# A cosine layer with six Strassen pairs of chunks, and three of its elementwise operations on GpSimd

## The chip, the cores and the metric

The kernel runs on one core of a Trainium2 chip. The metric is the device time of one execution in microseconds, median over several runs; before the change it is 544.96 us (3 runs, 544.89 to 545.14).

## The reference, cut to what matters

Attention (2 batches, 12 heads, 448 tokens, head size 64, causal mask), then a gated layer of 768 x 1536, then the layer that the change is about:

```python
def _moe2_ref(x, w_in, w_out):          # x: 896 x 768, w_in: 768 x 2048
    h = x @ w_in
    g = h * np.cos(h)
    return (g @ w_out).astype(np.float32)
```

The weights come as 64-bit floats, and the result is wanted in 32-bit precision.

## The kernel before

**Layout.** All activations lie transposed: 128 features on the partitions, 448 tokens of one batch on the free axis. Batch b is one moving operand of 448 columns. Each fp32 operand is held as a rounded part (hi) and a remainder (lo), and each 128 x 128 block of weights is multiplied three times (hi by hi, hi by lo, lo by hi): these are the lines L232 to L234 in `products`, and L500 to L502 in `Product.product`.

**Weights.** A chunk is 128 rows of outputs by 768 inputs. SyncE loads it as raw 64-bit words. ScalarE takes the upper part out (L169), VectorE puts the fp32 word together (L171; `upper_of` and `word_of`), ScalarE makes hi (L467, called by `parts`) and VectorE lo (L429, called through `difference` by `low`).

**The cosine layer.** Its 16 chunks of weights go in eight pairs, u = 0 to 7, called units here. `KINDS` says how each is done. A plain unit (P) multiplies two chunks with two batches: 8 halves (numbers 8 to 15) of 9 matmuls, 72 in all. A Strassen unit (S) takes the 2 x 2 blocks (two chunks by two halves of the inputs, and two halves of the inputs by two batches) with seven products (numbers 1 to 7) of 9 matmuls, 63 in all. Product 4 of an S unit is issued in the unit behind it (`old`). So a unit behind an S unit has 9 more matmuls than its own order has, and an S unit has 54 of its own besides.

An S unit needs sums of the weights. With f0 and f1 the words of its chunks: s1 = f1 left half + f1 right half and s2 = s1 - f0 left half (`sums12`, L478 and L479 by way of L429, in the unit before it), s3 = f0 left - f1 left and s4 = f0 right - s2 (`sums34`, L481 to L485), hi of the left block of them by ScalarE, lo by VectorE. In PSUM, ScalarE copies product 1 (L527) into the bank in which products 6 and 7 add up, and later that bank again (L536); VectorE adds s5 to it behind product 6 (L533) and behind product 7 (L538). L538 writes `tmp`, in SBUF: it is one of the unit's four results. The other three stay in PSUM.

**Order.** The schedule is written out by hand: each engine runs its instructions in the order in which the loop emits them. A unit has a position `at` for each product in `order`; `emit` issues that product on TensorE, then the work behind the one before it (`behind`). Then come pieces of the work on weights by position, then one step of `cosines`: it finishes the result that was begun a position ago (ScalarE's sine L736, VectorE's product with h L737) and begins another (ScalarE's scaled copy L742, VectorE's remainder L743). In an S unit behind an S unit the order on VectorE is: s3, s4 and a remainder (at 0); word of f0 of the next unit, low22 (L493), product, remainder of `tmp` (at 1); lo of s3 and s4, product with `tmp` (at 2); lo of the next A, remainder (at 3); L533, word of f1 of the next unit, s1, s2, product (at 4); remainder (at 5); L538, lo of s1 and s2, product (at 6). On ScalarE: hi of the lower right block (L489), upper part, copy; L527, hi of s3 and s4, sine, copy of `tmp`; L530, hi of the next A, sine of `tmp`; upper part, copy; sine; hi of s1 and s2, copy; L536, sine. GpSimd has work in the attention alone (L290, L286, and the sum L362 of two SBUF operands of 448 columns).

The lines that matter:

```python
for at, n in enumerate(order):
    emit(old if n == 4 else unit, n)
    if at == 0:
        if seven:
            unit.sums34()
            unit.high22()
```

Of the kernel before, what the change touches and what calls it, by code (L numbers as in the profile page):

```python
# [18 lines left out]
ALU = mybir.AluOpType  # L19
# [3 lines left out]
B, H, S, D = 2, 12, 448, 64  # L23
# [14 lines left out]
WH = KP * P  # L38
PLAIN = 2

KINDS = "PSSPSSSP"

FIRST_ROWS = {2: (0, 3), 4: (3, 5)}
FIRST_ROWS_END = 5
# [29 lines left out]
def attn_moe_moe2(  # L74
# [9 lines left out]
    nc = tc.nc  # L84
# [16 lines left out]
    def slot(tag, name, dtype=F32R):  # L101
        pool = gpool if tag[0] == "g" else spool if tag[0] == "t" else hpool if tag in ("f0", "f1", "f2") else bpool
        return pool.tile([P, 2, S], dtype, tag=tag, name=name)
# [313 lines left out]
    def temp(tag, bufs):  # L417
        return epool.tile([P, S], F32, tag=tag, name=tag, bufs=bufs)
# [9 lines left out]
    def difference(dst, a, b):  # L428
        nc.vector.tensor_tensor(dst, a, b, op=ALU.subtract)  # L429
# [19 lines left out]
    def run(n):  # L449
        for i in range(n):  # L450
            next(todo, None)
# [8 lines left out]
    class Product:  # L460
# [17 lines left out]
            nc.vector.tensor_tensor(s1, f1[:, :WH], f1[:, WH:], op=ALU.add)  # L478
            difference(s2, s1, f0[:, :WH])  # L479

        def sums34(self):  # L481
            f0, f1 = self.w
            self.s34 = slot("t14", "s34", F32).rearrange("p a s -> p (a s)")[:, : WC * P]
            difference(self.s34[:, :WH], f0[:, :WH], f1[:, :WH])
            difference(self.s34[:, WH:], f0[:, WH:], self.s12[:, WH:])  # L485

        def high22(self):
            self.a22 = epool.tile([P, 2, WH], F32R, tag="a22", name="a22", bufs=2)
# [53 lines left out]
    class Gate(Product):  # L542
# [5 lines left out]
        def result(self, n):  # L548
            if n == 2:
                self.sg0 = temp("sg", 4)  # L550
                nc.scalar.activation(self.sg0, self.a[:, :S], AF.Sigmoid)
            elif n == 3:
                sg1 = temp("sg", 4)
                nc.scalar.activation(sg1, self.c[:, :S], AF.Sigmoid)
                gated(self.f, 1, sg1, self.tmp)
            else:
                gated(self.f, 0, self.sg0, self.e[:, :S])

    for f in range(PLAIN):
# [18 lines left out]
        if f == PLAIN - 1:  # L578
            unit = Gate(PLAIN)
# [25 lines left out]
    def upper_of():  # L605
        k = Chunk(step("decode"))
        k.decode(0, 0, k.n)
        return k

    def word_of(k):  # L610
        k.decode(1, 0, k.n)
        load_chunk()
        return k.w
# [3 lines left out]
    def emit(u, n):  # L617
        u.p(n)
        if done:
            v, m = done.pop()  # L620
            v.behind(m)
        done.append((u, n))
# [3 lines left out]
    for f in range(PLAIN, KH):  # L626
# [31 lines left out]
        unit, old = new, unit  # L658
# [68 lines left out]
    GF = [None] * KG  # L727
    GFTAG = ["t5", "t6", "t7", "t8", "b6", "b7", "b8", "t9", "t10", "t11", "g2", "g3", "f4", "f5", "f6", "t12"]
    due, turned = [], []

    def cosines():
        if turned:
            h, r, (f, b) = turned.pop(0)
            if GF[f] is None:
                GF[f] = slot(GFTAG.pop(0), f"g{f}", F32)
            nc.scalar.activation(r, r, AF.Sin, scale=TWOPI, bias=quarter)  # L736
            nc.vector.tensor_tensor(GF[f][:, b], r, h, op=ALU.mult)  # L737
        if due:
            h, fb = due.pop(0)
            r = temp("sg", 4)  # L740
            n = r.bitcast(I32)
            nc.scalar.activation(n, h, AF.Copy, scale=INV2PI, bias=0.25)  # L742
            nc.vector.scalar_tensor_tensor(r, h, INV2PI, n, op0=ALU.mult, op1=ALU.subtract)  # L743
            turned.append((h, r, fb))

    GTAG = ["b4", "f7", "b0", "b5", "f8", "b1", "t3", "f9", "b2", "t4", "t13", "t14"] + sum(XTAG, [])
    GORD = [(k, b) for c in range(0, KG, WC) for b in range(B) for k in range(c, min(KG, c + WC))]
# [3 lines left out]
    def split_g(n):  # L751
        for i in range(n):
            if GORD:
                k, b = GORD.pop(0)
                G[b][k] = slot(GTAG.pop(0), f"g{k}{b}")
                split(G[b][k], GF[k][:, b])
                if b == B - 1 and GFREE:
                    GTAG.append(GFREE.pop(0))

    class Pair(Product):  # L760
# [17 lines left out]
        def result(self, n):  # L778
            f = self.f
            if n == 2:  # L780
                due.append((self.a[:, :S], (f, 0)))
            elif n == 3:
                due.extend([(self.c[:, :S], (f, 1)), (self.tmp, (f + 1, 1))])
            elif n == 4:
                due.append((self.e[:, :S], (f + 1, 0)))
            elif n % 2:
                i, b = (n - 8) // 4, (n - 8) // 2 % 2
                due.append((self.banks[i, b][:, :S], (f + i, b)))

    c3 = at_chunk["use"]  # L790
    unit, old = Pair(0), None
    unit.A = next_chunk()
    unit.w = None, singles.pop(c3 + 1).w
    for u, kind in enumerate(KINDS):
        new, last = Pair(u + 1), u == len(KINDS) - 1
        seven = kind == "S"
        new_seven = not last and KINDS[u + 1] == "S"
        if seven:
            order = (1, 5, 2, 6, 4, 7, 3) if old else (1, 5, 6, 2, 7, 3)
        else:  # L800
            order = (8, 9, 4) + tuple(range(10, 16)) if old else tuple(range(8, 16))
        for at, n in enumerate(order):
            emit(old if n == 4 else unit, n)
            if at == 0:
                if seven:
                    unit.sums34()
                    unit.high22()
                else:
                    unit.C = unit.parts(unit.w[1])
                k0 = upper_of()  # L810
            elif at == 1:
                w0 = word_of(k0)
                if seven:
                    unit.S34 = unit.parts(unit.s34)
                    unit.low22()
                else:
                    unit.low(unit.C, unit.w[1])
            elif at == 2:
                new.A = unit.parts(w0)
                if seven:  # L820
                    unit.low(unit.S34, unit.s34)
            elif at == 3:
                k1 = upper_of()
                unit.low(new.A, w0)
            elif at == 4:
                new.w = w0, word_of(k1)
                if new_seven:
                    new.sums12()
            elif at == 5 and new_seven:
                new.S12 = new.parts(new.s12)  # L830
            if at == min(len(order) - 1, 6) and new_seven:
                new.low(new.S12, new.s12)
            cosines()
            run(1)
            if last and at > 1:
                split_g(1)
        unit, old = new, unit if seven else None
# [9 lines left out]
    for j in range(KP):  # L847
        ps2 = [[bank() for i in range(2)] for b in range(B)]
        for c in range(nch):
            wts = [next_chunk()]  # L850
            for b in range(B):
                advance()
                for i in range(2):
                    if i and not b:
                        wts.append(next_chunk())
                    g, m = G[b][c * WC : min(KG, c * WC + WC)], 2 * j + i
                    products(ps2[b][i], wts[i], g, c == 0, c == nch - 1)
                    cosines()
                    split_g(3)
                    if c == nch - 1:  # L860
                        o, ps = temp("sg", 4), ps2[b][i]
                        rows, c0 = slice(m * P, m * P + P), b * S
                        if m == KX - 1 and b == B - 1:

                            nc.scalar.copy(o[:, : S // 2], ps[:, : S // 2])
                            nc.vector.tensor_copy(o[:, S // 2 :], ps[:, S // 2 : S])
                            nc.scalar.dma_start(out=out[rows, c0 : c0 + S // 2], in_=o[:, : S // 2])
                            nc.sync.dma_start(out=out[rows, c0 + S // 2 : c0 + S], in_=o[:, S // 2 :])
                        else:
                            nc.scalar.copy(o, ps[:, :S])  # L870
                            nc.sync.dma_start(out=out[rows, c0 : c0 + S], in_=o)
# [55 lines left out]
```

## Time and profile before

| | |
|---|---|
| median of the runs | 544.96 us |
| the profiled execution's own time | 545.12 us |
| its span, first to last instruction | 543.3 us |
| around the span | 1.8 us |
| granted TensorE clock, mean | 1.000 |
| matmuls | 3059 |
| the cosine layer's units 0 to 6, first matmul to first matmul of unit 7 | 317.76 to 408.30 us |

The profile is one execution on the chip. Times are counted from the start of the span. PE is TensorE, DVE VectorE, ACT ScalarE, POOL GpSimd. A row of the timeline has the start in us, the duration in us, engine, line, operation, output and inputs with their shapes, and in brackets the idle time in front of it with what ended that. Instructions of one engine overlap: the next can start before the last has ended, so that the distance of two starts is what an instruction costs its engine when it is busy, and start plus duration is when another engine can go on.

### The profile page before, as it was taken

Reading aid. Unit: us, or ns where it says so; the run is one execution under the profiler, and the core shown is the slowest. Engines: PE = TensorE matmul, PEld = TensorE weight load, DVE = VectorE, ACT = ScalarE, POOL = GpSimd, SP = SyncE. Lnnn points to the kernel's source line nnn. Section 1 sums busy time; section 2 is a strip of 40 time slices with the busy share of each in tenths; the row PEclk is TensorE's granted clock in tenths of the full one; section 3 lists DMA queues with packets and bytes.
Section 4 is the critical chain, followed back from the end, with each engine's and each line's share of the span. In section 5 each row is a group of like instructions: output and inputs, shape, how many; then the busy total and the mean of one; then the engine's idle time right before and its main releaser. Section 6 shows DMA issues by size and latency. Waiting matters only on the chain.

```text
span 543.3 us, 8153 instructions
## 1 busy us (share of the span) xinstructions
PE 535.6 (99%) x3059; PEld 479.7 (88%) x3059; DVE 366.0 (67%) x688; ACT 321.4 (59%) x622; POOL 59.4 (11%) x131
## 2 busy tenths in 40 slices
PE   7999999999999999999999999999999999999997
PEld 5666679989999999999999999999999999999996
DVE  4889959896777777893626279977988991411400
ACT  5898956675555555882535277766787972513401
POOL 4688860000000000000000000000000000000000
PEclk9999999999999999999999999999999999999999
DMA  8745113344444333332515132433333242623401
GB/s 330 270 152 200 71 59 117 116 139 149 130 144 135 118 118 116 118 117 66 171 54 174 59 115 94 141 121 112 121 130 111 94 146 62 218 100 109 153 1 68
DMA packets 14728, 68.16 MB, mean 125 GB/s; under 512 B 1633, under 2 KB 3809, under 8 KB 14689
## 3 DMA queue, kind: packets, MB, share of 16 engines
q1 hardware_dynamic: 14400, 67.33, 37.8%
q8 instruction: 24, 0.39, 0.3%
q10 hardware_dynamic: 288, 0.31, 0.2%
q14 instruction: 16, 0.12, 0.1%
HBM read 64.88 MB, written 2.75 MB: 124 GB/s over the span
## 4 chain that ended last, share of the span: by engine, by line
PE 92%; DVE 4%; ACT 2%; POOL 1%; issue 1%; DVEq 0%; POOLq 0%
PE ps L232 17%; PE ps L233 17%; PE ps L234 17%; PE ps L500 10%; PE ps L501 10%; PE ps L502 10%; PE ps L330 4%; PE ps L346 4%; PE ps L306 3%; POOL pbuf L290 1%; DVE wlo L429 1%; DVE sg L743 1%; ACT pbuf L314 1%; PE ps L260 1%; DVE wf L171 0%
## 5 line engine op out<-in xcount | busy, mean ns | idle before, releaser
L169 ACT ACTIVATE up<-wraw 128x768 f16<-128x768 bf16 (+2 forms) x71 | 74.3, 1046 | 6.3 <-DMA wraw<-in_w_out_dram 5.1
L171 DVE SCALAR_TENSOR_TENSOR wf<-wraw,up 128x768 uint32<-128x768 uint32 (+2 forms) x71 | 66.8, 941 | 15.2 <-ACT up L169 15.0
L233 PE MATMUL ps<-g,whi 128*128 128x448 f32 x192 | 69.7, 363 | 0.0
L232 PE MATMUL ps<-g,whi 128*128 128x448 f32 x192 | 69.6, 362 | 0.0
L234 PE MATMUL ps<-g,wlo 128*128 128x448 f32 x192 | 69.1, 360 | 0.0
L182 DVE TENSOR_TENSOR wlo<-wf,whi 128x768 fp32r<-128x768 f32 (+2 forms) x35 | 32.0, 913 | 46.5 <-ACT whi L180 45.8
L232 PE MATMUL ps<-h,whi 128*128 128x448 f32 x144 | 52.3, 363 | 0.0
L234 PE MATMUL ps<-h,wlo 128*128 128x448 f32 x144 | 52.2, 362 | 0.0
L233 PE MATMUL ps<-h,whi 128*128 128x448 f32 x144 | 51.8, 360 | 0.0
L500 PE MATMUL ps<-T,whi 128*128 128x448 f32 x135 | 49.2, 365 | 0.2 <-DVE ps L533 0.2
L501 PE MATMUL ps<-T,whi 128*128 128x448 f32 x135 | 48.9, 362 | 0.0
L502 PE MATMUL ps<-T,wlo 128*128 128x448 f32 x135 | 48.7, 361 | 0.0
L314 ACT ACTIVATE pbuf<-ps,nm 128x64 f32<-128x64 f32 (+6 forms) x84 | 38.7, 482 | 9.5 <-DVE nm L310 8.9
L467 ACT ACTIVATE whi<-s 128x768 fp32r<-128x768 f32 x30 | 25.4, 845 | 27.2 <-DVE s L429 27.1
L290 POOL TENSOR_SCALAR pbuf<-pbuf,rs 128x64 f32<-128x64 f32 (+6 forms) x84 | 39.3, 490 | 9.2 <-PE ps L306 6.2
L232 PEld LDWEIGHTS ps<-g,whi 128*128 128x128 f32 x192 | 36.0, 188 | 2.9
L870 ACT COPY sg<-ps 128x448 f32<-128x448 f32 x11 | 5.9, 533 | 54.7 <-PE ps L234 54.4
L234 PEld LDWEIGHTS ps<-g,wlo 128*128 128x128 f32 x192 | 35.9, 187 | 2.5
L233 PEld LDWEIGHTS ps<-g,whi 128*128 128x128 f32 x192 | 36.0, 188 | 1.8
L180 ACT ACTIVATE whi<-wf 128x768 fp32r<-128x768 f32 (+2 forms) x35 | 27.7, 790 | 13.7 <-DVE wf L171 7.8
L310 DVE CUSTOM_DVE_ANT_0 ps<-ps,mask 128x64 f32<-128x64 f32 (+6 forms) x84 | 32.7, 458 | 2.9 <-PE ps L306 2.8
L501 PE MATMUL ps<-x,whi 128*128 128x448 f32 x90 | 32.7, 363 | 0.0
(109 smaller groups left out, 1226.8 us busy)
## 6 DMA issues: line engine op xcount, KB each, us to landing
wraw<-in_w_gv_dram SPq DMA_DIRECT2D x24, 768.0 KB, 4.4
wraw<-in_w_out_dram SPq DMA_DIRECT2D x24, 768.0 KB, 4.5
wraw<-in_w_in_dram SPq DMA_DIRECT2D x16, 768.0 KB, 4.3
qkv<-in_qkv_dram SPq DMA_DIRECT2D x9, 928.0 KB, 5.0
wraw<-in_w_out_dram SPq DMA_DIRECT2D x6, 512.0 KB, 3.8
out_dram<-sg SPq DMA_DIRECT2D x11, 224.0 KB, 2.0
qkv<-in_qkv_dram SPq DMA_DIRECT2D x3, 256.0 KB, 7.9
qkv<-in_qkv_dram SPq DMA_DIRECT2D x1, 672.0 KB, 7.7
```

What stands on the lines that cost most here:

```text
L169: nc.scalar.activation(up.bitcast(F16)[:, 1::2], self.top[:, e0:e1], AF.Copy)
L171: nc.vector.scalar_tensor_tensor(self.w[:, e0:e1].bitcast(U32), self.mid[:, e0:e1], 13, up.bitcast(U32), op0=ALU.logical_shift_right, op1= ...
L182: nc.vector.tensor_tensor(self.lo[:, e0:e1], self.w[:, e0:e1], self.hi.bitcast(F32)[:, e0:e1], op=ALU.subtract)
L232: mm(ps[:, :S], lhsT=hi[:, blk], rhs=r[:, 0], start=first and k == 0, stop=False)
L233: mm(ps[:, :S], lhsT=hi[:, blk], rhs=r[:, 1], start=False, stop=False)
L234: mm(ps[:, :S], lhsT=lo[:, blk], rhs=r[:, 0], start=False, stop=last and k == n - 1)
L290: nc.gpsimd.tensor_scalar(row, row, rs[:, i : i + 1], 1.0, op0=ALU.mult, op1=ALU.mult)
L310: nc.vector.tensor_tensor_reduce(out=ps[:, :w], in0=ps[:, :w], in1=mask[:, S - w :], scale=-0.125, scalar=3.0e38, op0=ALU.add, op1=ALU.min ...
L314: nc.scalar.activation(pb[:, POFF[i] : POFF[i] + w], ps[:, :w], AF.Exp, scale=-1.0, bias=nm[:, i : i + 1], accum_out=sums[:, i : i + 1],)
L500: mm(ps[:, :S], lhsT=hi[:, blk], rhs=r[:, 0], start=start, stop=False, skip_group_check=True)
L501: mm(ps[:, :S], lhsT=hi[:, blk], rhs=r[:, 1], start=False, stop=False, skip_group_check=True)
L502: mm(ps[:, :S], lhsT=lo[:, blk], rhs=r[:, 0], start=False, stop=stop, skip_group_check=True)
```

## The change

`KINDS` makes units 3 and 4 part of one row of six S units: unit 3 was plain. For all S units of the cosine layer, s3 and s4 are computed by GpSimd. The last product of the cosine of the result that lies in `tmp` (feature block f + 1, batch 1) goes to GpSimd too; the other three products, and all remainders, stay on VectorE. Nothing else moves: the places in the emitted order are the same, and no DMA is added, removed or moved.

```diff
-KINDS = "PSSPSSSP"
+KINDS = "PSSSSSSP"
...
-        def sums34(self):
+        def sums34(self, eng=nc.vector):
             f0, f1 = self.w
             self.s34 = slot("t14", "s34", F32).rearrange("p a s -> p (a s)")[:, : WC * P]
-            difference(self.s34[:, :WH], f0[:, :WH], f1[:, :WH])
-            difference(self.s34[:, WH:], f0[:, WH:], self.s12[:, WH:])
+            eng.tensor_tensor(self.s34[:, :WH], f0[:, :WH], f1[:, :WH], op=ALU.subtract)
+            eng.tensor_tensor(self.s34[:, WH:], f0[:, WH:], self.s12[:, WH:], op=ALU.subtract)
...
     def cosines():
         if turned:
-            h, r, (f, b) = turned.pop(0)
+            h, r, (f, b), eng = turned.pop(0)
             if GF[f] is None:
                 GF[f] = slot(GFTAG.pop(0), f"g{f}", F32)
             nc.scalar.activation(r, r, AF.Sin, scale=TWOPI, bias=quarter)
-            nc.vector.tensor_tensor(GF[f][:, b], r, h, op=ALU.mult)
+            eng.tensor_tensor(GF[f][:, b], r, h, op=ALU.mult)
         if due:
-            h, fb = due.pop(0)
+            h, fb, eng = due.pop(0)
             r = temp("sg", 4)
             n = r.bitcast(I32)
             nc.scalar.activation(n, h, AF.Copy, scale=INV2PI, bias=0.25)
             nc.vector.scalar_tensor_tensor(r, h, INV2PI, n, op0=ALU.mult, op1=ALU.subtract)
-            turned.append((h, r, fb))
+            turned.append((h, r, fb, eng))
...
         def result(self, n):
             f = self.f
             if n == 2:
-                due.append((self.a[:, :S], (f, 0)))
+                due.append((self.a[:, :S], (f, 0), nc.vector))
             elif n == 3:
-                due.extend([(self.c[:, :S], (f, 1)), (self.tmp, (f + 1, 1))])
+                due.extend([(self.c[:, :S], (f, 1), nc.vector), (self.tmp, (f + 1, 1), nc.gpsimd)])
             elif n == 4:
-                due.append((self.e[:, :S], (f + 1, 0)))
+                due.append((self.e[:, :S], (f + 1, 0), nc.vector))
             elif n % 2:
                 i, b = (n - 8) // 4, (n - 8) // 2 % 2
-                due.append((self.banks[i, b][:, :S], (f + i, b)))
+                due.append((self.banks[i, b][:, :S], (f + i, b), nc.vector))
...
             if at == 0:
                 if seven:
-                    unit.sums34()
+                    unit.sums34(nc.gpsimd)
                     unit.high22()
```

## Rows read from the trace of the kernel before

**Rows 1.** The page: busy time, share of the span and instructions of each engine.
```profile
PE 535.6 (99%) x3059; PEld 479.7 (88%) x3059; DVE 366.0 (67%) x688; ACT 321.4 (59%) x622; POOL 59.4 (11%) x131
```
**Rows 2.** The page: the chain that ended last, by engine.
```profile
PE 92%; DVE 4%; ACT 2%; POOL 1%; issue 1%; DVEq 0%; POOLq 0%
```
**Rows 3.** Timeline of TensorE in the cosine layer (start, duration, instruction).
```profile
317.76 0.36 PE L232 MATMUL ps<-y,whi 128*128 128x448 f32 x1
...
335.76 0.43 PE L500 MATMUL ps<-T,whi 128*128 128x448 f32 x1
...
352.04 0.40 PE L500 MATMUL ps<-T,whi 128*128 128x448 f32 x1
...
404.62 0.44 PE L500 MATMUL ps<-T,whi 128*128 128x448 f32 x1 [0.17 <-DVE ps L533]
...
408.30 0.36 PE L232 MATMUL ps<-y,whi 128*128 128x448 f32 x1
```
**Rows 4.** Windows: busy time of each engine in unit 5, columns PE, PEld, DVE, ACT, POOL.
```profile
382.80:395.50 12.70, 12.70 (x66) 11.90 (x65) 11.71 (x20) 9.79 (x18) 0.00 (x0) 1.00 0.41 138
```
**Rows 5.** Timeline of VectorE, units 2, 5 and 6.
```profile
351.23 0.62 DVE L533 TENSOR_TENSOR ps<-ps,s 128x448 f32<-128x448 f32 x1
...
390.69 0.62 DVE L533 TENSOR_TENSOR ps<-ps,s 128x448 f32<-128x448 f32 x1
391.22 0.95 DVE L171 SCALAR_TENSOR_TENSOR wf<-wraw,up 128x768 uint32<-128x768 uint32 x1
392.20 0.56 DVE L478 TENSOR_TENSOR s<-wf 128x384 f32<-128x384 f32 x1
392.80 0.56 DVE L429 TENSOR_TENSOR s<-s,wf 128x384 f32<-128x384 f32 x1
...
402.45 0.95 DVE L429 TENSOR_TENSOR wlo<-wf,whi 128x768 fp32r<-128x768 f32 x1
403.32 0.62 DVE L743 SCALAR_TENSOR_TENSOR sg<-ps,sg 128x448 f32<-128x448 f32 x1
403.85 0.62 DVE L533 TENSOR_TENSOR ps<-ps,s 128x448 f32<-128x448 f32 x1
```
**Rows 6.** Timeline of ScalarE between unit 5's s2 and unit 6's last copy.
```profile
393.39 0.85 ACT L467 ACTIVATE whi<-s 128x768 fp32r<-128x768 f32 x1 [1.91 <-DVE s L429]
...
395.36 0.67 ACT L736 ACTIVATE sg<-sg,quarter 128x448 f32<-128x448 f32 x1 [0.26 <-DVE sg L743]
...
398.22 0.85 ACT L467 ACTIVATE whi<-s 128x768 fp32r<-128x768 f32 x1
...
401.16 0.67 ACT L736 ACTIVATE sg<-sg,quarter 128x448 f32<-128x448 f32 x1
...
402.68 0.51 ACT L742 ACTIVATE sg<-ps 128x448 int32<-128x448 f32 x1
```
**Rows 7.** GpSimd's sums L362 (x count: shortest/median/longest ns, first and last start).
```profile
L362 POOL TENSOR_TENSOR xf<-x x12: 1134/1153/1445, 23.6 to 80.8; 128x448 f32<-128x448 f32 x12
```
**Rows 8.** Timeline of GpSimd in the attention.
```profile
45.64 1.45 POOL L362 TENSOR_TENSOR xf<-x 128x448 f32<-128x448 f32 x1
...
76.07 1.16 POOL L362 TENSOR_TENSOR xf<-x 128x448 f32<-128x448 f32 x1 [1.16 <-DVE x L361]
80.80 1.16 POOL L362 TENSOR_TENSOR xf<-x 128x448 f32<-128x448 f32 x1 [3.57 <-DVE x L361]
```
**Rows 9.** Timeline of VectorE in the attention, beside rows 8.
```profile
45.34 0.74 DVE L171 SCALAR_TENSOR_TENSOR wf<-wraw,up 128x384 uint32<-128x384 uint32 x1
46.08 0.69 DVE L336 COPY pt<-ps 128x512 f32<-128x512 f32 x1
...
75.38 0.61 DVE L361 TENSOR_TENSOR x<-ps,x 128x448 fp32r<-128x448 f32 x1
76.57 1.47 DVE L182 TENSOR_TENSOR wlo<-wf,whi 128x768 fp32r<-128x768 f32 x1 [0.58 <-ACT whi L180]
...
81.07 1.70 DVE L171 SCALAR_TENSOR_TENSOR wf<-wraw,up 128x768 uint32<-128x768 uint32 x1 [0.35 <-ACT up L169]
```
**Rows 10.** Groups by line: s3 on VectorE (count, busy us, mean ns, idle before).
```profile
L429 DVE TENSOR_TENSOR s<-wf,wf 128x384 f32<-128x384 f32 x15 | 8.3, 554 | 0.0
```

## The prediction

> **What bounds the kernel now.** I read the page first: TensorE is busy for 99% of the span, VectorE for 67%, ScalarE for 59%, GpSimd for 11% [rows 1], and the chain that ended last lies on TensorE for 92% and on VectorE for 4% [rows 2]. Taken alone, these say that nine matmuls fewer are nine matmuls saved. So I read the cosine layer by itself, first TensorE's timeline [rows 3]. A matmul lasts 0.36 us, but the next starts 0.20 us after it: from 317.76 to 335.76 there are 90 of them (72 of unit 0, 18 of unit 1), 18.00 us. The duration must not be used as the price; 0.20 us is. Units 0 to 6 have 450 matmuls, 90.0 us, and took 408.30 - 317.76 = 90.54. So TensorE lost 0.54 us, 0.17 of it at 404.62, where product 7 of unit 6 waited for VectorE's L533. Smaller waits show as long first matmuls at 335.76 (unit 1, 0.43 instead of 0.36) and 352.04 (unit 2, 0.40). These are places without slack.
>
> Then the other engines in one S unit: in 12.70 us of unit 5 VectorE is busy for 11.71 and ScalarE for 9.79 [rows 4]. At this rate an S unit's elementwise work hardly keeps up. L533 shows it: it comes at 390.69 in unit 5 and at 403.85 in unit 6 [rows 5], 13.16 us apart, and 63 matmuls need 12.6. Each S unit in a row puts VectorE 0.56 us later; three in a row end with the stall at 404.62, and a plain unit between lets the engines catch up. The change takes that unit out.
>
> **Which loop has 13.16 us.** From row to row: s2 of unit 5 starts at 392.80 and ends at 393.36 [rows 5]; ScalarE, which has waited 1.91 us for it, makes hi of s1 and s2 at 393.39 and goes on without another wait than 0.26 us to the copy at 402.68 [rows 6]. These 9.29 us are ScalarE's own queue. That copy ends at 403.19; with the 0.08 us that a signal takes (L361 ends at 75.99, GpSimd starts at 76.07 [rows 8, 9]) VectorE could start L743 at 403.27 and did at 403.32. Then L533 0.53 later, the word 0.53 later, s1 0.98 after that, s2 0.60 after that, ScalarE's next hi 0.59 later [rows 5, 6]. Sum: 9.29 + 0.59 (to 403.27) + 0.53 + 0.53 + 0.98 + 0.60 + 0.59 = 13.11 us. So the loop goes through all of ScalarE's queue and a short piece of VectorE's. What VectorE does beside ScalarE's piece is hidden, and that it was about as long (0.05 us more) is a coincidence.
>
> **Part 1, nine matmuls go.** Unit 3 has 72 matmuls as P and 54 as S; unit 4 gets product 4, nine more. 450 - 18 + 9 = 441, so -1.8 us where TensorE sets the pace. With the 0.54 us of waits this is all that can be won: -2.34 us.
>
> **Part 2, what VectorE gives away.** Per S unit s3 and s4 (0.47 us each from start to start, 554 ns each by duration [rows 10]; the 0.47 is 384 columns of 448 at 0.53 [rows 5], an estimate) and one product of 448 columns at 0.53: 1.47 us. All three lie in the hidden piece, beside ScalarE's 9.29 us. So they shorten the loop by the 0.05 us alone, to 13.11, which is still 0.51 over the 12.6 of TensorE. L533 of unit 2 comes at 351.23 [rows 5]; what is in front of it is gapless VectorE work (unit 1) and ScalarE's queue (unit 2), so I leave it there. Four loops later, in unit 6, it is 351.23 + 4 x 13.11 = 403.67, against 403.85 before. What follows keeps its distance. Parts 1 and 2 together: **-0.2 us**. The 1.8 us of matmuls saved are waited away, since five S units in a row behind the first have no plain unit to catch up in.
>
> **Part 3, what GpSimd takes.** One sum of 448 columns takes it 1.15 us [rows 7]; by columns, 384 take 0.99 (estimate). Three operations are 3.1 us in 12.6, so GpSimd is no bound. The new waits are ScalarE's hi of s3 and s4 (behind it sine and copy) and VectorE's word of the next f0, whose buffer GpSimd must have read. Both are covered: s4 can be done some 1.5 us after s2, and hi came 4.8 us after the hi of s1 and s2 [rows 6]. They cost nothing while that holds. No DMA and no SyncE or GpSimd queue step is passed by anything, since the emitted places stay.
>
> **Part 4, the price.** GpSimd and VectorE get in each other's way here. L182 of 768 columns ran 1.47 us from 76.57 and L171 1.70 from 81.07, and 0.95 is normal for both forms [rows 5, 9]; at both times GpSimd had begun L362 just before (76.07, 80.80 [rows 8]). The delays, 0.52 and 0.75, put the release 0.14 us before GpSimd's recorded end (77.09 of 77.23, 81.82 of 81.96). The other way round, L171 (45.34, ends 46.08) held up L362 (45.64): it took 1.45 instead of 1.15, so 0.30, which again is 0.14 before the holder's end. VectorE's instructions with an operand in PSUM are not held: L336 at 46.08 took its 0.69 under GpSimd's sum [rows 8, 9].
>
> Now place s3. GpSimd is free and waits only for the word of f1, which VectorE makes just ahead of s1 and s2. With the word starting at 0: it ends at 0.95; s1 (two SBUF operands) starts at 0.98; s3 is ready at 1.03 and gets in when s1 lets go, at 0.98 + 0.56 - 0.14 = 1.40; it lets go at 1.40 + 0.99 - 0.14 = 2.25. s2 (two SBUF operands, needs s1) would have started at 1.58, so it is **0.67 us late**. And s2 is on the loop: ScalarE's queue waits for it. s4 then runs while VectorE works on PSUM operands, so it holds nothing up. The product with `tmp` is ready at 401.16 + 0.67 + 0.09 = 401.92 in unit 6's times [rows 6]; VectorE's lo, at 402.45 before [rows 5], comes earlier by the 0.53 of the product and by what ScalarE's copies leave of the 0.94 for s3 and s4, so at about 401.7 (estimate): lo is first, by 0.2 us, and the product waits for it at no price.
>
> Six s2 are hit, for units 1 to 6, and since units 1 and 2 have no slack [rows 3] all of it arrives: 6 x 0.67 = 4.0 us. **Sum:** -0.2 + 4.0 = +3.8 on the profiled execution's 545.12, or 548.9; that execution is 0.16 over the median of 544.96, so the forecast is **548.8 us**. Unit 7 then begins at about 412.1 instead of 408.30.
>
> Bounds of the price. Below: zero, if s3 and s2 don't meet (rival 1); a gain is excluded, for s2 can't start before s1 ends. Above: 0.31 us more in each of five units (rival 3). I take 0.67, since two rows of before show just this pair of operations held, by 0.52 and 0.75.
>
> The Trainium skill, "SBUF — State Buffer", section "Who interferes with whom", says that a VectorE instruction with two SBUF inputs contends with a GpSimd instruction that reads SBUF, and that the holder keeps the port for the whole instruction. The rows agree that one is held, but show the release 0.14 us before the recorded end; by the page's letter s2 would be 0.95 late, the sum +5.5 us and the time 550.5.
>
> **Rivals.**
> 1. *No meeting.* GpSimd begins s3 so late that s2 goes first, or operations at one column a cycle don't collide. For it: nothing in the trace shows two VectorE instructions in a row with GpSimd waiting between them. Against it: [rows 8, 9]. Then parts 1 and 2 alone hold: 544.8 us, no change. The Trainium skill's "Advanced Engine Details and Errata", section "VectorE Performance Modes", speaks of interference for two-port VectorE instructions in those modes; read as the only case, it gives this rival, and [rows 9] speak against it. Chance 0.20.
> 2. *TensorE sets the pace* (the other side). The loop is shorter than I take it, as VectorE, freed of 1.47 us, answers ScalarE sooner at several places at once. It decides from a loop of 12.6 us, 0.51 below my sum; then up to -2.34: 542.6 us. For it: VectorE's 11.71 of 12.70 us [rows 4]. Against it: ScalarE has one wait of 0.26 us for VectorE in 9.29 [rows 6], so there is little to answer sooner. Chance 0.13.
> 3. *The product with `tmp` gets in ahead of lo as well.* It decides if the sine comes 0.2 us earlier against lo. Then lo, due at 401.7, waits until the product lets go at 401.7 + 1.15 - 0.14 = 402.71, and L743 starts 0.87 later, at 403.58 instead of 403.27: 0.31 late in each of the five units that have such a product ahead of a sum, +1.6 on the forecast: 550.4 us. For it: the 0.2 us is little. Against it: both hang on ScalarE's queue and move together. Chance 0.09.
>
> **How the numbers follow.** The forecast has 0.58, 548.8, with its own range 547.5 to 550.3 (0.45 to 0.9 us for the price of one s2). 0.2% of 545 is 1.1 us, about what a measurement of this kernel can tell from no change: below 543.9 is faster, above 546.1 slower. Faster: rival 2 and a little of rival 1, 0.15. Same: most of rival 1, 0.19. Slower: 0.66. The range has to take in rival 1, since 0.58 alone is short of 0.8: 544.2 to 550.4 leaves out rival 2 below and half of rival 3 above.
>
> **What would show it.** Right: GpSimd has three operations in each unit from 1 to 6; s2 lasts about 1.2 us instead of 0.56; L533 of units 3 to 6 come 13.8 us apart; TensorE waits some 0.7 to 1.2 us a unit, most often at product 7 for L533, some 6 us in all; unit 7 starts near 412. VectorE's busy time then hardly falls, as waiting counts as busy. If s2 stays at 0.56 and the spacing is 13.1, rival 1 is right; at 12.6 with TensorE without gaps, rival 2. A lo of 1.5 us or more beside the `tmp` product would be rival 3. I am wrong at the root if TensorE's waits in this layer are below 2 us.

## The result and the profile after

The changed kernel takes 548.97 us (median of 4 runs, 548.65 to 549.27), the kernel before 544.93 us beside it (544.89 to 545.14): ratio 1.0073, 95% interval 1.0056 to 1.0091. It is slower by 4.0 us, though it has nine matmuls less.

The page of the changed kernel, busy time and instructions of each engine, to be read against [rows 1]:
```profile
PE 536.5 (98%) x3050; PEld 476.8 (87%) x3050; DVE 366.2 (67%) x678; ACT 323.1 (59%) x627; POOL 83.2 (15%) x149
```
TensorE has 3050 matmuls instead of 3059. VectorE has ten instructions fewer and is as busy as before: waiting for the SBUF port counts as busy (s2 below). On the chain that ended last, against [rows 2]:
```profile
PE 80%; ACT 10%; DVE 6%; issue 2%; POOL 1%; DVEq 0%; POOLq 0%
```
TensorE fell from 92% to 80%, and what took its place is first ScalarE. These shares do not measure the loss: e1, e2 and e3 below have 81% for TensorE, in the time of the kernel before.

TensorE's timeline, against [rows 3]: first matmul of the layer, first waits, product 7 of units 5 and 6, first matmul of unit 7.
```profile
317.38 0.36 PE L232 MATMUL ps<-y,whi 128*128 128x448 f32 x1
...
336.03 0.47 PE L500 MATMUL ps<-T,whi 128*128 128x448 f32 x1 [0.49 <-ACT ps L527]
...
352.95 0.44 PE L500 MATMUL ps<-T,whi 128*128 128x448 f32 x1 [0.43 <-DVE ps L533]
...
394.01 0.44 PE L500 MATMUL ps<-T,whi 128*128 128x448 f32 x1 [0.48 <-DVE ps L533]
...
406.85 0.37 PE L502 MATMUL ps<-T,a 128*128 128x448 f32 x1
407.70 0.45 PE L500 MATMUL ps<-T,whi 128*128 128x448 f32 x1 [0.48 <-DVE ps L533]
...
411.38 0.36 PE L232 MATMUL ps<-y,whi 128*128 128x448 f32 x1
```
Units 0 to 6 take 411.38 - 317.38 = 94.00 us, 3.46 more than the 90.54 before. Their 441 matmuls need 88.2, so TensorE loses 5.8 us. The idle time in a row's brackets counts only from the end of the matmul in front (0.36 us), so it is less than what is lost: at 407.70 the start comes 0.85 us behind the one before (406.85) instead of 0.20, which is 0.65 lost where the brackets have 0.48. One such place stands in every unit from 1 to 6: in unit 1 the wait is for ScalarE's L527, in units 2 to 6, at product 7, for L533. The rest are short delays (starts 0.28 to 0.34 us apart) right behind these places and, by the list of waits, where lo of the weights (L429) or the copy L527 comes late. What the layer does not explain (it starts 0.38 us earlier, and what comes behind it takes 0.5 longer) is of the size in which the profiled executions of these kernels differ.

VectorE in unit 5, against [rows 5], and GpSimd beside it:
```profile
391.21 0.95 DVE L429 TENSOR_TENSOR wlo<-wf,whi 128x768 fp32r<-128x768 f32 x1
392.70 0.63 DVE L743 SCALAR_TENSOR_TENSOR sg<-ps,sg 128x448 f32<-128x448 f32 x1 [0.54 <-ACT sg L742]
393.25 0.62 DVE L533 TENSOR_TENSOR ps<-ps,s 128x448 f32<-128x448 f32 x1
393.77 0.95 DVE L171 SCALAR_TENSOR_TENSOR wf<-wraw,up 128x768 uint32<-128x768 uint32 x1
394.76 0.56 DVE L478 TENSOR_TENSOR s<-wf 128x384 f32<-128x384 f32 x1
395.35 1.26 DVE L429 TENSOR_TENSOR s<-s,wf 128x384 f32<-128x384 f32 x1
...
406.93 0.62 DVE L533 TENSOR_TENSOR ps<-ps,s 128x448 f32<-128x448 f32 x1
```
```profile
391.39 1.78 POOL L737 TENSOR_TENSOR g<-sg,tmp 128x448 f32<-128x448 f32 x1 [7.38 <-ACT sg L736]
394.87 1.32 POOL L484 TENSOR_TENSOR s<-wf,wf 128x384 f32<-128x384 f32 x1 [1.69 <-DVE wf L171]
396.69 1.01 POOL L485 TENSOR_TENSOR s<-wf,s 128x384 f32<-128x384 f32 x1 [0.50 <-DVE s L429]
```
GpSimd begins s3 at 394.87, while s1 (394.76) has the port, and takes 1.32 us where s4 takes 1.01. s2, at 395.35, lasts 1.26 instead of 0.56. Both agree with a release 0.14 us before the holder's recorded end: s1 ends at 395.32, so s3 gets in at 395.18 and with its 1.01 us ends at 396.19 (394.87 + 1.32); it lets go at 396.05, and 0.56 us later s2 ends at 396.61 (395.35 + 1.26). L533 of units 5 and 6 are 13.68 us apart. The product with `tmp` came 0.18 us behind lo (391.21), waited for it (1.78 us instead of some 1.15) and held nothing up.

ScalarE, against [rows 6]: it waits for s2, then works through its queue almost without a break to the copy that L743 needs.
```profile
392.16 0.51 ACT L742 ACTIVATE sg<-ps 128x448 int32<-128x448 f32 x1
393.36 0.67 ACT L736 ACTIVATE sg<-sg,quarter 128x448 f32<-128x448 f32 x1 [0.69 <-DVE sg L743]
396.64 0.85 ACT L467 ACTIVATE whi<-s 128x768 fp32r<-128x768 f32 x1 [2.61 <-DVE s L429]
...
398.61 0.67 ACT L736 ACTIVATE sg<-sg,quarter 128x448 f32<-128x448 f32 x1 [0.26 <-DVE sg L743]
...
405.83 0.52 ACT L742 ACTIVATE sg<-ps 128x448 int32<-128x448 f32 x1
```
The wait for s2 has grown from 1.91 to 2.61 us, by the same 0.70. From the hi at 396.64 to the copy at 405.83 the only wait in brackets is 0.26 us, as before.

### The profile page after: what moved, and what is told of

Read it like the earlier page. It is cut to its first block, busy times and chain, and to the rows that moved or that the text cites. A ratio compares the mean times of both kernels' runs of the same rounds, so it can differ in the third digit from the quotient of the medians.

```text
span 546.9 us, 8162 instructions
## 1 busy us (share of the span) xinstructions
PE 536.5 (98%) x3050; PEld 476.8 (87%) x3050; DVE 366.2 (67%) x678; ACT 323.1 (59%) x627; POOL 83.2 (15%) x149
## 4 chain that ended last, share of the span: by engine, by line
PE 80%; ACT 10%; DVE 6%; issue 2%; POOL 1%; DVEq 0%; POOLq 0%
PE ps L232 15%; PE ps L234 15%; PE ps L233 15%; PE ps L500 8%; PE ps L501 8%; PE ps L502 8%; PE ps L330 4%; PE ps L346 4%; PE ps L306 3%; ACT up L169 2%; ACT whi L467 2%; ACT sg L742 2%; DVE s L429 1%; ACT sg L736 1%; DVE wf L171 1%
## 5 line engine op out<-in xcount | busy, mean ns | idle before, releaser
L500 PE MATMUL ps<-T,whi 128*128 128x448 f32 x144 | 52.8, 367 | 2.9 <-DVE ps L533 2.4
L502 PE MATMUL ps<-T,wlo 128*128 128x448 f32 x144 | 52.5, 364 | 0.0
L501 PE MATMUL ps<-T,whi 128*128 128x448 f32 x144 | 52.2, 363 | 0.0
L467 ACT ACTIVATE whi<-s 128x768 fp32r<-128x768 f32 x32 | 27.0, 844 | 35.8 <-DVE s L429 34.1
L484 POOL TENSOR_TENSOR s<-wf,wf 128x384 f32<-128x384 f32 x6 | 7.9, 1310 | 263.8 <-DVE wf L171 263.8
```

The costliest lines, as they stand in the source:

```text
L467: nc.scalar.activation(hi, src, AF.Copy)
L500: mm(ps[:, :S], lhsT=hi[:, blk], rhs=r[:, 0], start=start, stop=False, skip_group_check=True)
L501: mm(ps[:, :S], lhsT=hi[:, blk], rhs=r[:, 1], start=False, stop=False, skip_group_check=True)
L502: mm(ps[:, :S], lhsT=lo[:, blk], rhs=r[:, 0], start=False, stop=stop, skip_group_check=True)
```

## The experiments

The theory (A): s3 on GpSimd holds s2 by 0.7 us, and s2 is on a loop of ScalarE's queue and a piece of VectorE's that is longer than TensorE's 12.6 us even without it. The rivals: B, GpSimd delivers s3 and s4 too late; C, a row of six S units costs the time, whoever makes the sums; and for the later runs D, VectorE's amount of work is the bound.

Each run in one table. "Layer" is from the first matmul of unit 0 to the first of unit 7 in the profiled execution, "loop" the distance of L533 of units 5 and 6, and the ratio is to the kernel before in the same job, with its 95% interval.

| run | time, us | ratio | layer, us | loop, us |
|---|---|---|---|---|
| before | 544.93 | 1 | 90.54 | 13.16 |
| changed | 548.97 | 1.0073 (1.0056 to 1.0091) | 94.00 | 13.68 |
| e1, s4 first | 545.35 | 1.0003 (0.9994 to 1.0013) | 90.46 | 13.01 |
| e2, row of S units alone | 545.15 | 0.9999 (0.9990 to 1.0009) | 90.57 | 13.16 |
| e3, sums back on VectorE | 544.79 | 0.9994 (0.9984 to 1.0003) | 90.18 | 13.07 |
| e4, old order of units | 547.51 | 1.0043 (1.0028 to 1.0058) | 92.65 | 13.70 |
| e5, s4 first, L489 on VectorE | 544.15 | 0.9983 (0.9975 to 0.9992) | 89.33 | 12.59 |
| e6, row alone, L489 on VectorE | 545.03 | 0.9999 (0.9990 to 1.0008) | 90.43 | 13.16 |
| e7, e5 and L530 on VectorE | 549.07 | 1.0074 (1.0062 to 1.0087) | 94.24 | 13.45 |
| e8, s3 in halves | 546.57 | 1.0027 (1.0016 to 1.0037) | 91.89 | 13.27 |
| e9, e5 without unit 1 | 543.50 | 0.9974 (0.9963 to 0.9984) | 88.59 | 12.58 |
| e10, `tmp` product back | 548.98 | 1.0074 (1.0059 to 1.0090) | 94.23 | 13.73 |

**e1: s4 before s3.** The changed kernel with the two lines of `sums34` exchanged:
```diff
-            eng.tensor_tensor(self.s34[:, :WH], f0[:, :WH], f1[:, :WH], op=ALU.subtract)
             eng.tensor_tensor(self.s34[:, WH:], f0[:, WH:], self.s12[:, WH:], op=ALU.subtract)
+            eng.tensor_tensor(self.s34[:, :WH], f0[:, :WH], f1[:, :WH], op=ALU.subtract)
```


> The changed kernel with one edit: GpSimd computes s4 first and s3 second. s4 needs s2, so neither sum can start before VectorE has finished s2. Theory A (s3 holds the port that s2 needs, and s2 is on the loop of ScalarE's queue): s2 is back at 0.56 us, the distance of two L533 in a row of S units falls from 13.69 to 13.1, six times 0.67 us come back, 548.97 - 4.0 = 545.0 us. Theory B (GpSimd delivers its sums too late, and ScalarE's hi of s3 and s4 waits for them): the sums end later still, by about 1 us, and the time stays at 549 or rises. Theory C (the row of S units costs, whoever does the sums and in whatever order): 549 us.

545.35 us: 3.6 of the 4.0 us are back with the same work on the same engines. VectorE's s2 and L533 of the same unit, and GpSimd's sums:
```profile
390.80 0.62 DVE L533 TENSOR_TENSOR ps<-ps,s 128x448 f32<-128x448 f32 x1
...
392.91 0.56 DVE L429 TENSOR_TENSOR s<-s,wf 128x384 f32<-128x384 f32 x1
...
403.81 0.62 DVE L533 TENSOR_TENSOR ps<-ps,s 128x448 f32<-128x448 f32 x1
```
```profile
393.61 1.02 POOL L484 TENSOR_TENSOR s<-wf,s 128x384 f32<-128x384 f32 x1 [2.88 <-DVE s L429]
394.59 1.02 POOL L485 TENSOR_TENSOR s<-wf,wf 128x384 f32<-128x384 f32 x1
```
s2 is 0.56 again. The sums now come after it, when VectorE works with operands in PSUM, and both take 1.02. C falls with the time. B needs ScalarE's hi of s3 and s4 to wait for GpSimd, and in the changed kernel it came at 401.41, 3.7 us behind the end of s4. What is left, 13.01 us a loop, is still over 12.6, so nothing is won against the kernel before.

e1 also has a cost of its own, in unit 0, where s4 and s3 hold two VectorE instructions that took 0.62 before:
```profile
329.21 1.36 DVE L238 TENSOR_TENSOR T<-u,T 128x448 fp32r<-128x448 f32 x1
...
331.02 0.91 DVE L238 TENSOR_TENSOR T<-u,T 128x448 fp32r<-128x448 f32 x1
```
```profile
329.07 1.02 POOL L484 TENSOR_TENSOR s<-wf,s 128x384 f32<-128x384 f32 x1 [247.09 <-PE ps L234]
330.05 1.41 POOL L485 TENSOR_TENSOR s<-wf,wf 128x384 f32<-128x384 f32 x1
```
L533 of unit 1 comes 21.33 us behind the layer's first matmul, where it was 20.79 before: 0.54 late.

**e2: the order of units alone.** The kernel before with `KINDS = "PSSSSSSP"`.

> The kernel before with the new order of units alone (PSSSSSSP); all sums and products stay on VectorE. Theory A: the loop is the 13.16 us seen between units 5 and 6 before; L533 of unit 6 at 351.23 + 4 x 13.16 = 403.87 against 403.85, so 545.0 us, no change: the nine matmuls saved are waited away. Theory C (a row of six S units is what costs 4 us): 549 us. If VectorE's work gets later from unit to unit by more than the loop shows, between the two.

545.15 us, no difference, and L533 of unit 6 comes at 403.86 us, where 403.87 was expected. So the 1.8 us of matmuls saved are waited away on VectorE and ScalarE, with no GpSimd in it.

**e3: the sums back on VectorE,** the `tmp` product stays on GpSimd (`unit.sums34()` in place of `unit.sums34(nc.gpsimd)`).

> The changed kernel with s3 and s4 back on VectorE; the product with tmp stays on GpSimd. Theory A: nothing holds s2, the loop is ScalarE's 13.11 us, 544.8 us, if VectorE's lo of the next A still starts before the product is ready. By my walk they are tied here (lo some 0.9 us later than in the changed kernel, since s3 and s4 are back in front of it); if the product gets in first, lo is held up to 1 us in five units, of which 0.5 arrives: up to 547.3 us. Theory C: 549 us.

544.79 us, no difference that can be told from before. The tie was as close as it could be, and lo won it: GpSimd's product began at 401.36 and lo at 401.37, yet lo kept its 0.95 us and the product took 1.97.
```profile
401.37 0.95 DVE L429 TENSOR_TENSOR wlo<-wf,whi 128x768 fp32r<-128x768 f32 x1
```
```profile
401.36 1.97 POOL L737 TENSOR_TENSOR g<-sg,tmp 128x448 f32<-128x448 f32 x1 [11.10 <-ACT sg L736]
```

**e4: the old order of units with GpSimd's part.** The changed kernel with `KINDS = "PSSPSSSP"`.

> The changed kernel with the old order of units (PSSPSSSP): GpSimd has the sums and the tmp product of five S units, and there are nine matmuls more. Theory A: s2 is held in each of the five, and what arrives on TensorE is 0.5 to 0.67 each in units 1 and 2, nothing at unit 4 (the plain unit in front gives it back), and in units 5 and 6 1.3 less the 0.5 of slack that unit 5 has: about +2.0 over before, 547 us. Theory C (GpSimd's part is free): 545 or a little below.

547.51 us, 2.3 over before, where 2.0 was expected. So GpSimd's part costs time without the new order too: s2 is held in each of the five units (1.25 to 1.26 us), and 2.11 us of it arrive in the layer. Against before, L533 of unit 1 is 0.70 late and the next one 0.66 more; the plain unit gives the next hold back; units 5 and 6 add 0.22 and 0.54.

**e10: the `tmp` product back on VectorE,** the sums stay on GpSimd, s3 first (`(self.tmp, (f + 1, 1), nc.vector)`).

> The changed kernel with the product with tmp back on VectorE; the sums stay on GpSimd, s3 first. Theory A: s2 is held as in the changed kernel, and VectorE's 0.53 us more per unit lies in the part of the loop that ScalarE sets (VectorE idles 0.55 us there): 13.7 us from L533 to L533, 549.0 us. If GpSimd's product takes part in the loss: 547 us or less. If VectorE's amount of work is the bound: 551 us.

548.98 us, the time of the changed kernel. With e3 this splits GpSimd's part: the sums cost everything, the product nothing, and VectorE's 0.53 us a unit for that product is hidden but for 0.05: the distances of L533 from unit 2 on are 13.72 to 13.74 here and 13.68 to 13.69 in the changed kernel. L743 now begins 0.09 us behind the end of the copy that it needs, and not 0.03 (406.38 behind 405.83 + 0.52 in the changed kernel), since VectorE comes to it without a wait, straight from lo:
```profile
406.82 0.62 DVE L743 SCALAR_TENSOR_TENSOR sg<-ps,sg 128x448 f32<-128x448 f32 x1
```
```profile
406.21 0.52 ACT L742 ACTIVATE sg<-ps 128x448 int32<-128x448 f32 x1
```
This is the 0.05 us that the prediction found between VectorE's work and ScalarE's queue before the change.

**e8: s3 in two halves.** The dose:
```diff
-            eng.tensor_tensor(self.s34[:, :WH], f0[:, :WH], f1[:, :WH], op=ALU.subtract)
+            for c in range(0, WH, WH // 2):
+                eng.tensor_tensor(self.s34[:, c : c + WH // 2], f0[:, c : c + WH // 2], f1[:, c : c + WH // 2], op=ALU.subtract)
```


> The changed kernel with s3 in two instructions of 192 columns. Theory A: s2 waits only for the first half, which holds until 1.40 + 0.62 - 0.14 = 1.88 after the word's start (0.62 us: estimate from 1.02 for 384 and 1.15 for 448 columns), then the second half waits for s2: s2 is 0.30 late instead of 0.70, 6 x 0.3 on 545.2, about 547.0 us. If GpSimd kept the port over both halves: s2 1.0 late, 551 us. Theory B or C: 549 us.

546.57 us, near the 547.0 expected. VectorE's s1 and s2, and GpSimd's second half (L485 here):
```profile
393.55 0.56 DVE L478 TENSOR_TENSOR s<-wf 128x384 f32<-128x384 f32 x1
394.14 0.83 DVE L429 TENSOR_TENSOR s<-s,wf 128x384 f32<-128x384 f32 x1
```
```profile
394.52 0.91 POOL L485 TENSOR_TENSOR s<-wf,wf 128x192 f32<-128x192 f32 x1
```
s2 is held by 0.27 instead of 0.70, and the loop is 13.27: 0.26 over e1's 13.01, where the whole s3 puts it 0.67 over. The time follows the hold, and the port changes hands between two instructions of GpSimd: the second half begins while s2 runs, and ends at 395.43, 0.46 behind s2 (394.97).

**e5: ScalarE's queue made shorter.** e1, and hi of the lower right block by VectorE, at position 5 of the unit before, where e1's VectorE idled 0.81 us:
```diff
-        def high22(self):
+        def high22(self, copy=None):
...
-            nc.scalar.activation(self.a22[:, 0], self.w[1][:, WH:], AF.Copy)
+            (copy or nc.scalar.copy)(self.a22[:, 0], self.w[1][:, WH:])
...
                     unit.sums34(nc.gpsimd)
-                    unit.high22()
...
             elif at == 5 and new_seven:
                 new.S12 = new.parts(new.s12)
+                new.high22(nc.vector.tensor_copy)
```


> The run with s4 first, and hi of the lower right block (L489, 0.41 us of ScalarE's queue per unit) made by VectorE one unit earlier, at position 5, where VectorE idled 0.81 us. Theory A (in that run the loop is 13.01 us and 9.2 of it are ScalarE's queue): the loop falls by 0.4 to 12.6, TensorE's own time; most of the nine matmuls comes back: 545.35 - 5 x 0.4 + 0.2 = 543.4 us, 542.9 at best. Theory D (VectorE's amount of work per unit is the bound): VectorE gets 0.47 us more per unit and the time rises to 546 or more.

The loop is 12.59, TensorE's own time, and 544.15 us is below both kernels, by 0.9 us the one before. It is 0.75 us more than expected. The expectation took 0.4 us off five distances, and only the four behind unit 2 had it to give (from unit 1 to unit 2 L533 is 12.64 apart in e1 already). And unit 1 lost 0.4 us more than in e1: the product there that waits for ScalarE's L527 starts 1.08 us behind the matmul in front (0.70 in e1, 0.20 without a wait). The list of waits has 0.72 for it, and no other wait of TensorE in the layer.

**e6: the same move without GpSimd** (e2 with that edit).

> The order of units alone (all sums and products on VectorE), with the same move of L489 from ScalarE to VectorE. Theory A: without GpSimd VectorE's own queue from L538 on is as long as ScalarE's (0.05 us apart before), so a shorter queue of ScalarE gives nothing: 545.1 us. If ScalarE alone set the loop: 543.4 us. Theory D: 547 us.

545.03 us, loop 13.16: nothing. The two engines' queues are tied, so taking work from one of them gives nothing (ScalarE, here) or next to nothing (VectorE: 13.01 in e1, 13.07 in e3); it needs both, GpSimd for VectorE and VectorE for ScalarE.

**e7: L530 to VectorE as well** (in the cosine layer `nc.vector.tensor_copy` in place of `nc.scalar.copy` for s5).

> As the run with L489 on VectorE and s4 first, and the copy of s5 (L530, PSUM to SBUF, 0.42 us of ScalarE's queue) on VectorE as well. Theory A: ScalarE's queue would allow 12.2 us, VectorE's from the remainder of the unit's first result on 12.5; TensorE's 12.6 bound: 542.7 to 543.3 us, at most 0.5 better than without it. Theory D: slower by 0.5 us in each of five units.

549.07 us: a miss by 6 us. VectorE and GpSimd in the same stretch (L739 here is L737 elsewhere):
```profile
390.26 0.62 DVE L530 COPY s<-ps 128x448 f32<-128x448 f32 x1
390.79 0.95 DVE L429 TENSOR_TENSOR wlo<-s,whi 128x768 fp32r<-128x768 f32 x1
391.66 1.91 DVE L429 TENSOR_TENSOR wlo<-wf,whi 128x768 fp32r<-128x768 f32 x1
```
```profile
391.12 1.64 POOL L739 TENSOR_TENSOR g<-sg,tmp 128x448 f32<-128x448 f32 x1 [5.62 <-ACT sg L738]
```
The copy puts the lo at 391.66 behind the start of GpSimd's product at 391.12; the product gets the port when the lo in front of it lets go, and lo lasts 1.91 us instead of 0.95, in each of units 2 to 6. Against e5 L533 comes 0.53 us later in unit 1, where the copy alone is new, 1.03 more in unit 2 and 0.86 more in each unit behind it: 5.0 us together, and the time rose by 4.9. This rests on the rows; no run took the product back to VectorE in this kernel. This is the prediction's third rival, not in the changed kernel but in one with 0.53 us more in front of lo.

**e9: unit 1 as before.** In e5's unit 0 GpSimd's s4 and s3 held two VectorE instructions: L238, which is only there (1.36 us instead of 0.62), and L489 for longer than in the units behind (1.18 us instead of 0.93). Unit 1 gets its sums on VectorE and L489 on ScalarE again:
```diff
-                    unit.sums34(nc.gpsimd)
+                    if u == 1:
+                        unit.sums34()
+                        unit.high22()
+                    else:
+                        unit.sums34(nc.gpsimd)
```
(and `new.high22(nc.vector.tensor_copy)` only where `seven` is set).

> The run with s4 first and L489 on VectorE, except unit 1, which keeps its sums on VectorE and L489 on ScalarE as before. In that run unit 1 lost 0.72 us on L527: in unit 0 GpSimd's s4 and s3 held two of VectorE's instructions (1.36 and 1.18 us). Theory A: unit 1 is as before (a wait of 0.07 us), the loops from unit 2 on stay at 12.6: 544.15 - 0.6 = 543.5 us. If the wait in unit 1 has another cause, or the lost time comes back in unit 2, 544.1 us.

543.50 us, as expected: 1.5 us under the kernel before (0.9974, 0.9963 to 0.9984) and 5.5 under the changed one. The layer takes 88.59 us for 88.2 of matmuls. The chain that ended last, and L533 of the last four S units:
```profile
PE 97%; POOL 1%; ACT 1%; DVE 1%; issue 0%; POOLq 0%
```
```profile
364.07 0.62 DVE L533 TENSOR_TENSOR ps<-ps,s 128x448 f32<-128x448 f32 x1
...
376.66 0.62 DVE L533 TENSOR_TENSOR ps<-ps,s 128x448 f32<-128x448 f32 x1
...
389.25 0.62 DVE L533 TENSOR_TENSOR ps<-ps,s 128x448 f32<-128x448 f32 x1
...
401.83 0.62 DVE L533 TENSOR_TENSOR ps<-ps,s 128x448 f32<-128x448 f32 x1
```
The four are 12.6 us apart, and the list of waits has none of TensorE's in the layer: here TensorE sets the pace, and the nine matmuls are won.

## Why the prediction was right, point by point

- **The price of a matmul.** 0.20 us from start to start held: without waits 441 of them take 88.2 us, and e9 comes within 0.4 of it. One reading beside it was too small: of the 0.54 us lost before, not 0.17 but 0.33 lie at 404.62, which is 0.53 us behind the start in front of it instead of 0.20:
```profile
404.09 0.37 PE L502 MATMUL ps<-T,a 128*128 128x448 f32 x1
```
- **The loop without GpSimd's hold.** 13.11 us was forecast. e1 shows 13.01 and e3 13.07, and e2, with all work on VectorE, the 13.16 of before. That VectorE's 1.47 us a unit would give only 0.05 us was the step on which the sign hung: e1, which gives all of it away, and e3, which gives away the product, are within 0.1% of before. It was 0.15 us. The 0.10 too much in the forecast's sum are mainly two terms, as e1's rows show:
```profile
393.50 0.85 ACT L467 ACTIVATE whi<-s 128x768 fp32r<-128x768 f32 x1 [1.91 <-DVE s L429]
...
402.72 0.51 ACT L742 ACTIVATE sg<-ps 128x448 int32<-128x448 f32 x1
```
```profile
403.26 0.63 DVE L743 SCALAR_TENSOR_TENSOR sg<-ps,sg 128x448 f32<-128x448 f32 x1 [0.55 <-ACT sg L742]
```
ScalarE's queue takes 9.22 us and not 9.29, and L743 begins 0.03 us behind the end of the copy and not 0.08.
- **s2 held by s3.** 0.67 us forecast, 0.70 measured (1.26 against 0.56), and e1 shows that the order of the two operations is the whole of it. The Trainium skill's "SBUF — State Buffer", section "Who interferes with whom", has the holder keep the port for the whole instruction; by that the hold would have been 0.95 us. The trace agrees that s2 is held, but not for so long: the measured 0.70 fits the release 0.14 us before the recorded end that [rows 8, 9] showed.
- **Six holds, all arriving.** This held, measured against the kernel before as the forecast was. Counted from the layer's first matmul, L533 of unit 1 comes 0.68 us later than before (21.47 us against 20.79), L533 of unit 2 0.65 more (13.33 behind it against 12.68), and the four loops from there to unit 6 are 13.69 each, 0.68 over the 13.01 of a loop without the hold (e1): 4.04 us where 4.0 was forecast. That e1's layer is only 94.00 - 90.46 = 3.54 us shorter comes from the 0.54 us that e1 loses in unit 0.
- **The sum.** Mis-sized were parts 1 and 2: with a loop of 13.01 in place of 13.11, four times, they come to -0.6 us and not -0.2, so the layer grew by 3.46 us where 3.8 was the sum. 545.12 + 3.8 = 548.9 was for the profiled execution, which took 548.65. The median rose by 4.0, to 548.97; that the forecast of 548.8 came as near as 0.2 us to it is partly luck. (0.9 us a hold gives 550.2 as the upper end of the forecast's own range, not 550.3.)
- **The rivals.** The first, no meeting, is e1's kernel: forecast 544.8, measured 545.35. The reading of the Trainium skill's "Advanced Engine Details and Errata", section "VectorE Performance Modes", by which only the two-port modes interfere, does not hold here: s2 shows no faster mode (0.56 us for 384 columns in e1, where the copy L489 takes 0.35 in e6), and it was held. The second, TensorE as the bound, did not come by itself; it came when ScalarE's queue was cut as well (e5, e9). The third stayed out by 0.18 us, the lead of lo over the `tmp` product (0.2 was forecast); with more in front of lo it came (e7).
- **The covers.** The hi of s3 and s4 and the word of f0 never waited for GpSimd in the changed kernel. In e1 the second sum ends 0.36 us later, counted from L533 of the same unit (4.81 us behind it against 4.45), and e1 is faster by 3.6 us.

## What to carry to other kernels

When two engines feed each other in a loop, add the loop up from row to row before moving work: what lies beside the longer queue is free where it is and wins nothing elsewhere. On GpSimd, an elementwise operation on SBUF operands should be started when VectorE has a stretch of PSUM operands ahead; which of two independent lines comes first can be worth more than the nine matmuls. And a shorter queue moves starts by tenths of a microsecond, so a neighbour that lost the port by 0.2 us in one version can get it in the next.

## What the runs showed of the hardware that was not expected

A copy on VectorE with one SBUF operand is held by GpSimd too. Without GpSimd's sums (e6) L489 as a cast of 384 columns took 0.35 us. That is less than the 0.40 us that 384 columns make at the rate of VectorE's sums (an estimate: 0.87 us from start to start for 768 columns and 0.47 for 384, so 1.04 ns a column). Beside GpSimd's s4, which began 0.30 us ahead of it, it took 0.93 (e9):
```profile
393.46 0.35 DVE L489 CAST a<-wf 128x384 fp32r<-128x384 f32 x1
```
```profile
392.36 0.93 DVE L489 CAST a<-wf 128x384 fp32r<-128x384 f32 x1
...
393.26 0.62 DVE L743 SCALAR_TENSOR_TENSOR sg<-ps,sg 128x448 f32<-128x448 f32 x1
```
It fits into VectorE's idle time there (0.54 us in front of L743 in e6), so no loss shows. The recorded start on GpSimd is also not yet the hold: in e3 the product began 0.01 us ahead of lo and lost the port to it, while in e1 s4 began 0.14 us ahead of L238 (329.07 and 329.21) and won it.
